# A linear-attention and channel-mixing kernel: weight conversion without clamps, a range test on a second load of the weights, and a new order table

## The chip, the cores and the metric

The kernel runs on one core of a Trainium2 chip. The metric is device time in microseconds (us) of one execution, median of the runs. Five engines take part: TensorE (PE, matmuls; PEld is its weight load), VectorE (DVE), ScalarE (ACT), GpSimd (POOL) and SyncE (SP), which here only issues DMAs. Every engine works through its own queue in order; semaphores hold an instruction until what it needs is there, and all that stands behind it on that engine waits too.

## What is computed

A decaying outer-product state per head, then two mixing layers per batch:

```python
for t in range(S):
    cur = np.einsum('bhd,bhe->bhde', u[None] * kt, vt)
    y[:, :, t] = np.einsum('bhd,bhde->bhe', rt, state + cur)
    state = wt[:, :, :, None] * state + np.einsum('bhd,bhe->bhde', kt, vt)
# x: y laid out as (B, S, H * D)
xt = x.transpose(0, 2, 1)
h = xt @ U @ V
u = x + h.transpose(0, 2, 1)
ch = np.maximum(u @ w_ch1, 0.0) @ w_ch2
return u + ch
```

Batch 4, 8 heads, 768 steps, head size 48, width 384, hidden width 1536, rank 32. U, V, w_ch1 and w_ch2 come to the device as 64-bit floats and are turned into pairs of float32r values (a high and a low part) on the device.

## The kernel before

**The recurrence** is cut into 24 chunks g of 128 steps (four batches of six). For a chunk: DMAs load w, r and k (`rk`), v and, from batch 1 on, a second layout of r and k (`kr`). DVE scans the decays backwards (step F) and forwards (step Q), scales r and k by them (RP and KS, on DVE or POOL) and forms the u term (PR; from batch 1 RK, RU and RED). ACT or POOL spread that term on a diagonal (SEL, lines 445 and 447). PE makes the scores (AM, line 507), DVE merges them with the diagonal under a mask (CP, line 510), PE turns k (KT), adds to the state (DS), and writes y (YA lines 566 and 576, YZ lines 589 and 593). ZA and ZM (lines 538, 547, 549) carry the state Z from chunk to chunk. XE, XT and XN bring y into the two layouts that follow.

**The mixing** of a batch needs all its six chunks: PE sums them with U (`gb`), ACT and DVE split that sum (GS, then GSL at line 668), and PE adds the product with V to x, giving u for two blocks of 384 steps (`hp`, line 723). u is split into a high and a low part (lines 735 to 741). Then per block 12 UP groups (line 782, nine matmuls each into one of three PSUM tiles of the tag `ffn`), a ReLU that splits the hidden value (HH line 789 on ACT or 791 on DVE, HL line 795 on DVE), 12 DN groups (line 817), the sum with u (line 832) and the store.

**The weights.** Each of the 24 pieces of w_ch1 and w_ch2 (128x384, 384 KB as 64-bit floats) goes through one of seven `raw` tiles: the load, AB (line 247, ACT: magnitude of the upper word), E (line 260, ACT: lower word), C1 (line 264, DVE: clamp to the range that can be converted), C2 (line 271, DVE: shift), SG (sign; line 279 on ACT or 281 on DVE), ADD (line 288, DVE or POOL: the float32 value), HI (line 329 or 331) and SUB (line 336, DVE or POOL). U and V take the same way once each. The `raw` tiles are also what u is written to.

**The order.** Every step is listed in a table, `ORDER`, three characters a step: which step comes next, whether it runs on its second engine, and how many warm-up matmuls (line 178, 52 instructions in all, on scratch data) PE gets in front of it. The program is issued in that order, so the table sets each engine's queue, SP's too. Tile pools are small: two for w, four for `rk`, two for v, seven for `raw`.

**Range tests.** GUARD (line 411, ACT, with an accumulated output) and the totals of the decay test w. Shortly before the end their results are summed (lines 955 to 964) and all engines branch: inside the range the kernel is done, outside it a slow general path computes everything anew. The inputs timed here stay inside.

Of the kernel before, what the change touches and what calls it, by code (L numbers as in the profile page):

```python
# [39 lines left out]
def channel_order():  # L40
# [14 lines left out]
    "0W00c05T00X05U05P05Y14K10d00f03i03n00V04904N03t03j05V03p00Y10Z04L10a03q00g01b03u11c00e00h10K00F04O00b1110120"
    "4Z01301A03vM3w04Y04P03r03s01J03-00M00i00l05W13m03o11404z01e01500G01f03x11C01L03y00j04i10k14b03zG3+0161170400"
    "1d04h01g11h04+01t01801914104jC1K01M05604k043G4404g01i04n04T05714o04d04204e04a05p00L00N01j14f04l00n04m14c10O0"
    "1N05004U01u01w04Q05801O15904R01P15204p84q02900P14544604V04W65301Q01R14S11v01B04X01x01y13l05q05z14uC5514r24v0"
    "5y05405+06945s05E05A01D00Q05B14w01E05x10R00S05-04s02R01S08O05u05114t05F01F11k05v00m00o06A04-01G15C05D06015d6"
    "5e05J65w00p08R01z06115Z01H01I10q15G20r11+08T01-08Y05a18o05H02A06228X05b15c02006305K08y05Q05L04x04y02C05t18U0"  # L60
    "8Z00s00t02S05fC2B01U05h05I06B02D05M22T05g05N02E15i01T08P08z15r08a15j08p08b05k05l09h05m01V08W18V08Q06C02I09O0"
    "8r02a08c11W02U08t05n05o06408d16506602F02V08g08u01X18q06701Y06802W16D08v06E06F06G08+02K06H09g00I08e08f08x06I0"
    "6M01Z08S16J08-06N00J02X16R06S08w09208h09309008i02Y19409j08s18j06O06P06K06L06V02Z06T06U08k06Q09609P11a09F07M0"
    "1l07N02J02c09101n02L02M09508l02G02H01o06r06s06t02N12O16c06d02P09l06e09E02Q06W06X00u09G09Q19R01m06o06Y06p09H0"
    "9m09n19I12102306Z06a00v06q06b02200x09706u06v06w09J00y09K09p07101p17201q09L09q06l06m00w02s07302400z10+09M09r1"
    "6f01r01s16g06h0AY06n00-01019s09t09o19W09S19T09X09909A09B02512b0Ai02d0Ab02-02e09U0AZ06+0261270281AG02j09812t0"
    "9V0Ad02v06i06x02f0Ae0Aj16j02w06k09b09c09Y09y02g0Ag19i09w09u09v12u02x17406y09d0750Af09z0A109Z09k19a0D40A202h0"
    "2i02k02m09x02n09N02y12z0Ao09+02+16z0380Ak13903B03C09-06-0DU07009e02l02o12p12q12r03003203107O07Q0Ac1760A603Z0"
    "Al0330Am03A09f03D17U07707V03H03J0A90AB0A70780AE19C09D07903413507A07B0Ah0360370An13E03F07C07R07D07S13I07T1A80"
    "3b03a0Ap07E07F0AM03G07G03Q03c07W07P0Aa0AA17X17e08003d03K0AC0AD03L0D303M0AN08103R0AH1AI03N08203O07f1AO0AQ03e1"  # L70
    "3P08m08n0AJ07g03T03U03S03V0830D60DD0AF0DT0840850AK1AL13f03W13X13Y07H03g1E307b07c1DE1A017h07i17j0AP03h07I07J0"
    "7K0DW07L07k07l07m07q0E40DB0D71D807r17s07t0D90A30E507d07Y0E607u17v0AR0AS0Db1DA1DY0DZ0DF0DG0A40DC0A50Dd0De1Dv0"
    "EV0AT0AU0AV0DX17Z07a0D50Dc0Da0Df1DL0Aq0Ar0As0AW0AX0DH1DI1Dy0DM07z0DJ0DK0EL07n07w07x0EM0D+07o1Dg0At0Au0Dl0DN0"
    "7p0Av0Aw0Ax0D-0DV0Dw0E017+17-0DP07y0E20Ay0Az0860870A+0A-0B00B10B20B30B40B51B60EO0Hu0En0Ew0880B70E70Dz08908C0"
    "8D08E08A08B0C10B80EW1B91EQ0EU0ER0EP18F08G0Dh1Di0Dm0C20FD0Dj0EX1E80EY0C30BA18I0E108J08K0BZ0Dx0FN0ES1Ba0Bb0Dk0"
    "8L08M08N0Eo0BH0BI0BJ0BK08H0C50BN0C60C71DQ0E90EA0BL1BM0BQ0DO0ET1BO1BP0Dn0Eq0EB0EC0Ev0BR1Do0BS0Dq0Dr0Ds0F10BB0"
    "BC1C90Bf0CA0F20Ed0EZ1Es0FO0Bg1Bh0EG0Et0Dp1EH0ED0EN0Hl0CB1BD0CC0Eb0BE0Bi0Bc0BF1EE0BG0EF0Bl0Eu0EI0Ec0FM0Bj1Bk0"
    "FG0I80Ea1Ee0BW0BX0EJ0EK0FI0Ef0FE0F30BY0Ep0Eg0Ei0FP0Ej0FF0FQ0FR1FS1DR0DS0Bd0BT0BU1Er0BV0FJ0FK1Bm0Bn0Be0Bo0Hk0"
    "FH0Hn0Ht0Br0Bp0Ex0Ey1Hv0Hw0Hs0Bs0Bt0Dt0Hp0Bu0C41Ez0E+0Bx0By0Bq0Hq0Hr0Bz0Hx0Ik0C81CP0CQ0FL0IB0E-0B+0F00I90IG0"
    "ID0Bv0Bw0IE0CR0F40B-0Ce0CM0CN1Cf1CO0Du0Cg0F50FT0FU0II0C00IJ0IK0IO0IP0Cb0Ia0Ek0Cc0CG0CH1CI0Eh0F60F70CV0Il0Im1"  # L80
    "CJ0CK0H+0H-0CL0F80F90IC0I00IL0Ib0IA0JA0JB0Ij0FA0Cd0IF0FV0FW0Hy1FB0FC0Hz1Id0CY0CZ0Ca0Ii0CW0CD0CE0CF0IH0Ck0Cl0"
    "If0Ig0Cm0El0Em0CS0Ih1J10FX0Ch0FY0I10Ie0CT0CU0FZ0Hm0I20Fa0Fb0Ci1Cj0IQ0I30IM0CX0I40IS0IN0JC1IR0Fc0Is0Fd0In0Io0"
    "Cn0Fe0Ff0Jc0J00J30J81Gi0JS0Ic0J41IT0IU0J50Gj0Co0Cp0Cq0Ct0Fg0Cu0J60Fh0Fi0Fj1Cv0Cw0Fk0Cr0Cs0Cz0Ip0It0Fl0Fm0Fo0"
# [959 lines left out]
```

## Time and profile before

| | us |
|---|---|
| median of 3 runs | 460.49 |
| lowest, highest | 459.89, 461.44 |
| the profiled execution | 460.15 |
| its span, first to last instruction | 458.4 |
| lies around the span | 1.75 |

The profile is one execution. "Busy" is the time in which an engine had an instruction under way; neighbouring instructions overlap a little, so what one costs its queue is the distance from its start to the next start, which the chain of waits shows directly. The profiled execution is 0.34 us under the median.

### The profile page before, as it was taken

Reading aid. Unit: us, or ns where it says so; the run is one execution under the profiler, and the core shown is the slowest. Engines: PE = TensorE matmul, PEld = TensorE weight load, DVE = VectorE, ACT = ScalarE, POOL = GpSimd, SP = SyncE. Lnnn points to the kernel's source line nnn. Section 1 sums busy time; section 2 is a strip of 40 time slices with the busy share of each in tenths; the row PEclk is TensorE's granted clock in tenths of the full one; section 3 lists DMA queues with packets and bytes.
Section 4 is the critical chain, followed back from the end, with each engine's and each line's share of the span. In section 5 each row is a group of like instructions: output and inputs, shape, how many; then the busy total and the mean of one; then the engine's idle time right before and its main releaser. Section 6 shows DMA issues by size and latency. Waiting matters only on the chain.

```text
span 458.4 us, 9721 instructions
## 1 busy us (share of the span) xinstructions
PE 442.2 (96%) x4066; PEld 409.9 (89%) x4066; DVE 296.7 (65%) x529; ACT 175.1 (38%) x434; POOL 104.5 (23%) x99
## 2 busy tenths in 40 slices
PE   4998899999999999999999999999999999999996
PEld 3675668999999899899999799999998899999995
...
GB/s 271 378 133 216 281 238 61 177 288 160 147 76 127 180 62 115 67 90 82 147 42 167 59 61 64 20 123 54 23 18 1 1 17 19 2 39 31 0 3 54
DMA packets 20497, 46.95 MB, mean 102 GB/s; under 512 B 2400, under 2 KB 8928, under 8 KB 20448
## 3 DMA queue, kind: packets, MB, share of 16 engines
...
q8 instruction: 33, 0.54, 0.5%
...
## 4 chain that ended last, share of the span: by engine, by line
PE 85%; DVE 7%; ACT 3%; DMA 2%; issue 1%; SPq 1%; DVEq 0%; ACTq 0%
PE f L782 33%; PE f L817 33%; PE aps L507 4%; PE y L566 2%; PE trk L495 2%; PE y L576 2%; PE trx L626 2%; PE y L589 1%; PE dS L517 1%; DMA rk<-in_rkT 1%; DVE A L510 1%; PE hp L723 1%; PE ga L649 1%; DVE Q L395 1%; PE idle L178 1%
## 5 line engine op out<-in xcount | busy, mean ns | idle before, releaser
L782 PE MATMUL f<-u,w1h 128*128 128x384 f32 x576 | 150.1, 341 | 0.7 <-ACT xT L745 0.7
L782 PEld LDWEIGHTS f<-u,w1h 128*128 128x128 f32 x576 | 103.7, 188 | 1.3 <-ACT xT L745 1.0
L817 PE MATMUL f<-hh,w2h 128*128 128x384 f32 x288 | 99.1, 344 | 0.0
L782 PE MATMUL f<-u,w1l 128*128 128x384 f32 x288 | 97.5, 339 | 0.0
L817 PE MATMUL f<-hh,w2l 128*128 128x384 f32 x288 | 97.4, 338 | 0.0
L817 PE MATMUL f<-hl,w2h 128*128 128x384 f32 x288 | 97.0, 337 | 0.0
L795 DVE SCALAR_TENSOR_TENSOR hl<-f,hh 128x384 fp32r<-128x384 f32 x96 | 52.4, 553 | 41.0 <-ACT hh L789 39.8
L789 ACT ACTIVATE hh<-f 128x384 fp32r<-128x384 f32 x47 | 23.1, 494 | 142.7 <-PE f L782 142.6
L817 PEld LDWEIGHTS f<-hh,w2h 128*128 128x128 f32 x288 | 54.1, 188 | 1.2 <-DVE hl L795 0.6
L817 PEld LDWEIGHTS f<-hl,w2h 128*128 128x128 f32 x288 | 54.5, 189 | 0.4
L782 PEld LDWEIGHTS f<-u,w1l 128*128 128x128 f32 x288 | 54.0, 188 | 0.0
L817 PEld LDWEIGHTS f<-hh,w2l 128*128 128x128 f32 x288 | 54.0, 187 | 0.0
L791 DVE TENSOR_SCALAR hh<-f 128x384 fp32r<-128x384 f32 x49 | 27.1, 554 | 33.4 <-PE f L782 33.4
L832 DVE TENSOR_TENSOR xT<-f,xT 128x384 f32<-128x384 f32 x24 | 13.0, 550 | 36.9 <-PE f L817 36.9
L510 DVE COPY_PREDICATED A<-maskf,aps 128x1024 f32<-128x1024 uint32 x24 | 32.7, 1361 | 2.8 <-PE aps L507 2.4
L445 ACT ACTIVATE A<-ident,dv 128x128 f32<-128x128 f32 x108 | 34.0, 394 | 1.2 <-DVE dv L435 1.2
L382 DVE TENSOR_TENSOR_SCAN F<-w,resets 128x517 f32<-128x517 f32 x24 | 30.7, 1281 | 4.4 <-DMA w<-in_wT 4.4
L395 DVE TENSOR_TENSOR_SCAN Q<-w,qd 128x516 f32<-128x516 f32 x24 | 31.1, 1295 | 0.2
L741 POOL TENSOR_TENSOR u<-xT,u 128x384 fp32r<-128x384 f32 x9 | 10.3, 1153 | 82.9 <-DVE u L737 63.8
L507 PEld LDWEIGHTS aps<-rk 48*128 48x128 f32 x384 | 23.3, 187 | 5.6 <-issue 3.9
L507 PE MATMUL aps<-rk 48*128 48x128 f32 x384 | 27.9, 285 | 0.5 <-DMA raw_w<-in_w 0.4
L407 POOL TENSOR_TENSOR rk<-rk,F 128x512 f32<-128x512 f32 x13 | 17.1, 1317 | 47.4 <-DVE F L382 27.5
...
## 6 DMA issues: line engine op xcount, KB each, us to landing
...
raw_w<-in_w SPq DMA_DIRECT2D x24, 384.0 KB, 5.5
kr<-in_rkN SPq DMA_DIRECT2D x18, 384.0 KB, 3.9
...
```

Of the source, the lines that this page charges most:

```text
L382: nc.vector.tensor_tensor_scan(out=F[:, ::-1], data0=st["w"][:, ::-1], data1=resets[:, ::-1], initial=1.0, op0=ALU.mult, op1=ALU.add)
L395: nc.vector.tensor_tensor_scan(out=st["Q"], data0=st["w"][:, 0:n], data1=qd, initial=0.0, op0=ALU.mult, op1=ALU.add)
L407: ENG[eng].tensor_tensor(out=rk[:, 1], in0=rk[:, 1], in1=F5, op=ALU.mult)
L445: nc.scalar.activation(A[:, i, j], ident, AF.Copy, scale=dv[:, NP * i + j : NP * i + j + 1])
L507: nc.tensor.matmul(aps[:, i, j, :], rk[r, 1, j, :], rk[r, 0, j, :], start=True, stop=True)
L510: nc.vector.copy_predicated(flat(st["A"]), mask8, flat(st["aps"]))
L782: nc.tensor.matmul(ps, wt[:, f, ct, :], u[ct][:, z], start=(n == 0), stop=(n == 8))
L789: nc.scalar.activation(hh, d["ps", f], AF.Relu)
L791: nc.vector.tensor_scalar(out=hh, in0=d["ps", f], scalar1=0.0, scalar2=None, op0=ALU.max)
L795: nc.vector.scalar_tensor_tensor(out=hl, in0=d["ps", f], scalar=0.0, in1=hh.bitcast(F32), op0=ALU.max, op1=ALU.subtract)
L817: nc.tensor.matmul(d["o", ct], wt[:, 4 * ct + part, f - 3 * part, :], hid[f][z], start=(part == 0 and n == 0), stop=(part == 3 and n == 8),)
L832: nc.vector.tensor_tensor(out=o, in0=d["o", ct], in1=o, op=ALU.add)
```

## The change

The 24 weight pieces lose step C1: `c1 = ab if not clamped`, so C2 follows AB. U and V keep it. Instead, each piece is loaded a second time later in the run (LC, SP, into a `raw` tile) and two ACT instructions with accumulated outputs (RT) sum up its magnitudes, and what they lack to the lower bound, into `sums`. The DN group 3.1.1.0, the eighth from the end, comes after all tests. The final vote gets two more columns: one reduction and two comparisons on DVE more. The general path converts the weights again with the clamps. And the order table is new: it moves steps on every engine, chooses other second engines, and asks for 63 warm-up matmuls.

```diff
 ORDER = (
-    "4704A04G00000100304804C00704B10200400514D04H10603k00800A05O04F10905X00B00C15R04IG4J04MA0D00H80EO5S14E00T00U0"
...
+    "4V04e04Y05m00000105p05v04W04a00300204b04600400514f14gS5r04c04d10S00T00V00U00605s04Z10700800A00a00904h00W10b0"
...
+    two = const.tile([P, 1], F32, name="two")
+    nc.vector.memset(two, 2.0)
...
-    def split_raw(key):
+    def split_raw(key, exact=False):
...
-        c1 = step(
+        clamped = exact or kind in ("U", "V")
+        c1 = ab if not clamped else step(
             "C1 " + nm, "DVE",
             lambda: nc.vector.tensor_scalar(
                 out=d["a"], in0=d["a"], scalar1=2.0, scalar2=122880.0 * 65536.0, op0=ALU.max, op1=ALU.min
...
+    sums = const.tile([P, 2, 2 * NF], F32, name="sums")
+
+    def test_raw(kind, i):
+
+        d, nm, braw = {}, f"{kind}{i}", Buf("raw")
+        q = i + (kind == "w2") * NF
+
+        def load():
+            t = stage.tile([P, TB, 2], U32, tag="raw", name=f"again_{kind}_{i}", bufs=RAW_BUFS)
+            nc.sync.dma_start(t.rearrange("p n t -> p (n t)"), (w1 if kind == "w1" else w2)[i].bitcast(U32))
+            d["high"] = t.bitcast(F32)[:, :, 1]
+
+        def sizes():
+            x = d["high"]
+            nc.scalar.activation(x, x, AF.Abs, scale=2.0**16, accum_out=sums[:, 0, q : q + 1])
+            nc.scalar.activation(x, x, AF.Relu, scale=-1.0, bias=two, accum_out=sums[:, 1, q : q + 1])
+
+        l = step("LC " + nm, "SP", load, ready[kind, i], take=[braw])
+        tests.append(step("RT " + nm, "ACT", sizes, [l], use=[braw]))
...
-        step("GUARD " + nm, "ACT", check_w, [lw], use=[buf["w"]])
+        tests.append(step("GUARD " + nm, "ACT", check_w, [lw], use=[buf["w"]]))
+        tests.append(st["tots"])
...
+                last = tests if nm == "3.1.1.0" else []
                 prev = step(
-                    "DN " + nm, "PE", down, [prev] + [s for f in fs for s in hs[f][1:]] + ready.get(("w2", 4 * ct + part), []),
+                    "DN " + nm, "PE", down, last + [prev] + [s for f in fs for s in hs[f][1:]] + ready.get(("w2", 4 * ct + part), []),
...
+        for key in pieces[2:]:
+            split_raw(key, exact=True)
...
+    for key in pieces[2:]:
+        test_raw(*key)
...
+        nc.vector.tensor_reduce(out=per[:, 2:4], in_=sums, op=ALU.add, axis=AX.X)
...
+        nc.vector.tensor_scalar(out=per[:, 2:3], in0=per[:, 2:3], scalar1=122880.0 * 65536.0, scalar2=None, op0=ALU.is_lt)
+        nc.vector.tensor_scalar(out=per[:, 3:4], in0=per[:, 3:4], scalar1=0.0, scalar2=None, op0=ALU.is_le)
```

Lines of the changed kernel are shifted by some 25, so 668 becomes 694, 741 becomes 767 and so on.

The first place is DVE's queue from GSL of batch 0 (out `gs`) up to the last low part of u that the first UP needs. Before:

```order
L668 TENSOR_TENSOR gs<-gb,gs 32x384
L435 TENSOR_REDUCE dv_994<-kr_769 128x8
L317 TENSOR_TENSOR Vst<-vm_187,Vst 32x384
L510 COPY_PREDICATED A_890<-maskf,aps_940 128x1024
L331 CAST w2h<-cva_w_3_788 128x384
L382 SCALAR_TENSOR_TENSOR F_1031<-w_976,resets 128x517
L549 TENSOR_TENSOR Z_1034<-dS,tots 128x384
L741 TENSOR_TENSOR u_0_1_1036<-hp_0_1_988,u_0_1_1036 128x384
L741 TENSOR_TENSOR u_0_0_992<-hp_0_0_974,u_0_0_992 128x384
L741 TENSOR_TENSOR u_0_2_1043<-hp_0_2_999,u_0_2_1043 128x384
```

and after (L432 is KS of chunk 7, L575 ZM, L753 the sum for block 1, L763 and L767 the split of u, L773 the copy that frees a PSUM tile):

```order
L694 TENSOR_TENSOR gs<-gb,gs 32x384
L432 TENSOR_TENSOR rk_816<-rk_816,F_903 128x512
L575 TENSOR_TENSOR Z_1039<-dS,tots 128x384
L753 TENSOR_TENSOR xT_1_761<-hp_1_0_1030,xT_1_761 128x384
L763 CAST u_0_0_1053<-hp_0_0_896 128x384
L767 TENSOR_TENSOR u_0_0_1053<-hp_0_0_896,u_0_0_1053 128x384
L773 COPY xT_0_411<-hp_0_0_896 128x384
L767 TENSOR_TENSOR u_0_1_1063<-hp_0_1_1057,u_0_1_1063 128x384
L767 TENSOR_TENSOR u_0_2_1084<-hp_0_2_1068,u_0_2_1084 128x384
```

The reduction, the sum for V, the merge, a cast and the scan F have left the stretch; KS, the sum for block 1 and the split of the first u have come in.

The second place is SP's queue for chunks 3 and 5 (first number in a name: the chunk, or the piece of the weights). Before:

```order
L367 DMA v_0_320<-in_vN 128x448
L355 DMA w_3_324<-in_wT 128x517
L359 DMA rk_3_362<-in_rkT 128x1024
L237 DMA raw_w1_11_364<-in_w1 128x768
L367 DMA v_2_446<-in_vN 128x448
L355 DMA w_5_448<-in_wT 128x517
L237 DMA raw_w2_1_514<-in_w2 128x768
L373 DMA u_rep_116<-in_uB 128x384
L359 DMA rk_5_547<-in_rkT 128x1024
```

and after:

```order
L380 DMA w_5_373<-in_wT 128x517
L240 DMA raw_w1_0_427<-in_w1 128x768
L392 DMA v_1_445<-in_vN 128x448
L384 DMA rk_3_466<-in_rkT 128x1024
L240 DMA raw_w1_3_468<-in_w1 128x768
L392 DMA v_3_490<-in_vN 128x448
L240 DMA raw_w1_8_513<-in_w1 128x768
L240 DMA raw_w2_1_515<-in_w2 128x768
L392 DMA v_2_528<-in_vN 128x448
L384 DMA rk_5_594<-in_rkT 128x1024
```

The load of w for chunk 5 now stands in front of v of chunk 1 and `rk` of chunk 3; before, `rk` of chunk 3 and v of chunk 1 were issued ahead of it.

The third place is ACT's queue in the second block of batch 1, where ReLUs (`hh`) stand among other work. Before:

```order
L789 ACTIVATE hh_1_1_8_3054<-f1_1_1_8_3040 128x384
L789 ACTIVATE hh_1_1_2_3097<-f1_1_1_2_3087 128x384
L499 ACTIVATE kn_18_3105<-trk_18_3100 128x512
L411 ACTIVATE junk_114,guard_112<-w_20_3050,b_max_106 128x512
L609 ACTIVATE xT_2_1_3052<-y_16_3108 128x3x128
```

and after (L360 and L361 are the two halves of a test RT):

```order
L815 ACTIVATE hh_1_1_8_2922<-f1_1_1_8_2893 128x384
L360 ACTIVATE again_w2_4_2926,sums_125<-again_w2_4_2926 128x384
L361 ACTIVATE again_w2_4_2926,sums_125<-again_w2_4_2926,two_112 128x384
L360 ACTIVATE again_w1_0_2602,sums_125<-again_w1_0_2602 128x384
L361 ACTIVATE again_w1_0_2602,sums_125<-again_w1_0_2602,two_112 128x384
L815 ACTIVATE hh_1_1_2_2935<-f1_1_1_2_2903 128x384
```

Two tests, each behind a load of its own, have come between two ReLUs.

## Rows read from the trace of the kernel before

**Rows 1.** The page: busy time, share of the span and instructions of each engine.

```profile
PE 442.2 (96%) x4066; PEld 409.9 (89%) x4066; DVE 296.7 (65%) x529; ACT 175.1 (38%) x434; POOL 104.5 (23%) x99
```

**Rows 2.** Busy us (count) by stretch: PE PEld DVE ACT POOL, clock, DMA share, GB/s.

```profile
0.00:20.00 20.00, 13.51 (x76) 9.62 (x76) 17.48 (x38) 14.38 (x36) 2.28 (x8) 1.00 0.90 328
...
7.84:66.38 58.54, 53.65 (x704) 39.28 (x704) 56.97 (x102) 54.23 (x135) 19.46 (x15) 1.00 0.72 252
...
74.00:453.00 379.00, 378.96 (x3261) 364.26 (x3262) 227.61 (x403) 112.25 (x278) 78.00 (x72) 1.00 0.24 76
```

**Rows 3.** Warm-up matmuls up to 74 us, both sizes (busy, mean ns).

```profile
L178 PE MATMUL idle<-w2l 128*128 128x512 f32 x43 | 16.1, 481 | 3.8 <-DVE w2l L172 3.8
...
L178 PE MATMUL idle<-w2l 128*128 128x256 f32 x9 | 3.1, 339 | 0.0
```

**Rows 4.** The chain of waits, 66 to 97 us: start, length, engine, line.

```profile
66.38 0.57 DVE gs L668
...
67.43 0.65 PE hp L715 x2
68.08 0.17 PE hp L723
...
71.36 0.94 DVE u L741 x2
...
73.58 0.39 ACT xT L745
...
74.02 2.04 PE f L782 x10
...
91.94 4.77 PE f L782 x27
```

**Rows 5.** The same chain, 40 to 45 us: steps of DVE's queue.

```profile
40.92 0.60 DVE rk L402
41.53 1.15 DVE F L382
42.67 0.25 DVE cva_w L264
42.93 0.47 DVE cva_w L288
...
44.26 0.47 DVE Z L538
```

**Rows 6.** The timeline, DVE 39 to 58 us, and one POOL instruction beside it.

```profile
39.63 0.69 DVE L463 TENSOR_TENSOR kr<-rk 128x512 f32<-128x512 f32 x1 [1.43 <-DMA rk<-in_rkT]
...
48.68 0.36 DVE L271 TENSOR_SCALAR cva_w<-cva_w 128x384 uint32<-128x384 uint32 x1
...
54.28 0.95 DVE L549 TENSOR_TENSOR Z<-Z,tots 128x384 f32<-128x384 f32 x1
55.15 1.17 DVE L271 TENSOR_SCALAR cva_w<-cva_w 128x384 uint32<-128x384 uint32 x1
56.24 1.33 DVE L510 COPY_PREDICATED A<-maskf,aps 128x1024 f32<-128x1024 uint32 x1
57.46 0.54 DVE L538 TENSOR_TENSOR Z<-dS,Z 128x384 f32<-128x384 f32 x1
...
54.79 1.31 POOL L428 TENSOR_TENSOR kr<-kr 128x384 f32<-128x384 f32 x1
```

**Rows 7.** Waits of SP's queue up to 76 us (total, times, longest).

```profile
SPq L355 <- DVE Q L395: 12.0, 6, 3.2
```

**Rows 8.** DMA issues, 100 to 400 us: count, size, median us from issue to landing.

```profile
raw_w<-in_w SPq DMA_DIRECT2D x3, 384.0 KB, 5.0
```

**Rows 9.** ACT's groups of instructions (busy, mean ns, idle before).

```profile
L789 ACT ACTIVATE hh<-f 128x384 fp32r<-128x384 f32 x47 | 23.1, 494 | 142.7 <-PE f L782 142.6
...
L411 ACT ACTIVATION_READ_ACCUMULATOR junk<-w,b_max 128x1 f32 x24 | 4.7, 196 | 0.0
```

More of the change, by code (lines that the diff above doesn't have):

```diff
@@ L53 @@
 ORDER = (
-    "4704A04G00000100304804C00704B10200400514D04H10603k00800A05O04F10905X00B00C15R04IG4J04MA0D00H80EO5S14E00T00U0"
[L55 to L83, printed above, removed]
@@ new lines @@
+    "4400c00X00Y04F04905n05w10d04i14A10Z14804B05t04kW4l04504G14w00B04C00e10f04D04E15304x00C10D00y00z00-02K04j11C0"
+    "0g04HI4I04J05L01401E04m60+04z04-04n01011101600h05415200EW4L24M05004+14K11S04NC4O00F01201311U01D04701i01k00HA"
+    "6B05105O01F01T01V01j01l01G05505604R44S04P04Q15u10K00M059A1m11W01H05q15A01I04X04r20I05M00i04s64t05V11X01Y01J1"
+    "5N06E05W05X00L04o04p01K01y05716F15815Q04y04u04v05Y05P11Z15T10j06K05R01n05BY5C04q00k06G05Z15D04T04U00N05S10l0"
+    "0m10n16H06C06L15U01+05E01M00G00J05GC5c06MG6N10o01o06J05a05b05d05F10O01p16I06X06O00p18m08p05H05I05-01506001z0"
@@ new lines @@
+    "Kb0Kd0Kc0Ke0Hj03-0Ht0Kf0Kg0Kh0Hu0Hw0Hx0Ki0Kj0Kn0Hy0Hz0Kk0Kl0Ko0Kp0Kq0H+0Hv0H-0Kr0Ks0I00I10I20Kt0Ku0Km0L20L30"
+    "L40L80L91LA0LH0L50L61L70I30I403z0Ky0LI0LJ0K-0L01L10KP0Kv0Kw0LQ03d0LR0Kz1Kx0K+0LB0LC0LD0LN0LO1LE0LF0LP0LT0LG0"
+    "Ll0Lm0LS0Ln1LU0LK0LL0410Lp0Lq0LM0LV0LW0LZ0La0Lb0Lo0LX0Lt0Lu0Lc0Lf0Lg0Ld0Lh0Lr1Lv0Li0Lw1Le0Ls1MD0ME1MF0Lj0MM0"
+    "M40M51M10M60M21M30Lk0MP0LY0MQ1MR0M70M80M90MA0MN0MO0MG0MH0Lx0MB1MC0Ly1Lz0L+0L-0M00MJ0MV0MW0MK1ML0MS0MI0MT0MX0"
+    "MU0MY0Mb0Mc0Md0Me0Mf0Mh0Mi0MZ0Mg0I50Mj0Mk0Ml0Ma0Mm0"
@@ L339, in split_raw @@
         ready[key] = [hi, sub]
+    sums = const.tile([P, 2, 2 * NF], F32, name="sums")
[12 more added lines that the diff above has]
+        tests.append(step("RT " + nm, "ACT", sizes, [l], use=[braw]))
+    tests = []
     sts = {}
@@ L904, in general @@
         del steps[:], ups[:], keeps[:]
+        for key in pieces[2:]:
+            split_raw(key, exact=True)
+        for s in steps:
+            s.run()
+        del steps[:]
         with tc.For_i(0, B, 1) as b:
@@ L949, in rwkv_moe_kernel @@
         spare.left += 1
-    per = const.tile([P, 2], F32, name="per")
+    per = const.tile([P, 4], F32, name="per")
     low = const.tile([1, 1], F32, name="low")
@@ L956, in test @@
         nc.vector.tensor_reduce(out=per[:, 1:2], in_=tots, op=ALU.min, axis=AX.XY)
+        nc.vector.tensor_reduce(out=per[:, 2:4], in_=sums, op=ALU.add, axis=AX.X)
         nc.vector.tensor_scalar(out=per[:, 0:1], in0=per[:, 0:1], scalar1=0.0, scalar2=None, op0=ALU.is_le)
         nc.vector.tensor_scalar(out=per[:, 1:2], in0=per[:, 1:2], scalar1=DECAY_MIN, scalar2=None, op0=ALU.is_ge)
+        nc.vector.tensor_scalar(out=per[:, 2:3], in0=per[:, 2:3], scalar1=122880.0 * 65536.0, scalar2=None, op0=ALU.is_lt)
+        nc.vector.tensor_scalar(out=per[:, 3:4], in0=per[:, 3:4], scalar1=0.0, scalar2=None, op0=ALU.is_le)
     def vote():
         cnt = psT.tile([P, NP, P], F32, tag="tr", name="cnt")
-        nc.tensor.matmul(cnt[0:1, 0, 0:2], ones, per, start=True, stop=True)
-        nc.vector.tensor_reduce(out=low, in_=cnt[0:1, 0, 0:2], op=ALU.min, axis=AX.X)
+        nc.tensor.matmul(cnt[0:1, 0, 0:4], ones, per, start=True, stop=True)
+        nc.vector.tensor_reduce(out=low, in_=cnt[0:1, 0, 0:4], op=ALU.min, axis=AX.X)
         nc.vector.tensor_scalar(out=flag, in0=low, scalar1=P - 0.5, scalar2=None, op0=ALU.is_lt)
```

40 lines of the change are left out of this document (30 added, 10 removed).

## The prediction

> **What bounds the kernel now.** The page's busy shares come first and mislead: PE is busy 96% of the span [rows 1], which seems to leave nothing to gain. The windows by stretch show two kernels in one [rows 2]. From 74 to 453 us PE is busy 378.96 of 379.00 us: matmuls stand end to end, and no other engine is waited for. Up to 74 us PE looks busy too, but 52 of its instructions there are warm-up matmuls on scratch data, 16.1 + 3.1 = 19.2 us of it [rows 3]; the first UP cannot start before batch 0 has gone through its recurrence. There DVE is the bound: between 7.84 us, where its first PR starts, and 66.38 us, where GSL starts, it is busy 56.97 of 58.54 us, and ACT 54.23 [rows 2]. The chain of waits agrees: DVE up to GSL, then a relay of PE, ACT and DVE to the first UP at 74.02 us [rows 4].
>
> So the time is three terms: when the first UP starts, the matmuls that are left then, and a tail behind them, the sum and the store of the last tile, that the change leaves alone. I count the PE instructions in front of the first UP in both programs: besides the warm-ups they are the same, but for one XT (three transposes, 0.33 us on the chain) that now comes earlier. What PE has left shrinks by 0.33 us, and all else must come from the start of the first UP.
>
> **C1 and what fills its place.** 12 of the 24 C1 stood in DVE's queue before GSL. A C1 costs its queue 0.25 us [rows 5], so 12 x 0.25 = 3.0 us leave the bound. The other 12 lie under the dense matmuls, where DVE is busy 227.61 of 379 us [rows 2], and are worth nothing. But the new table does not hand these 3.0 us over; it spends them. Counting DVE's steps before GSL in both orders: three RP and one KS go to POOL or behind GSL (4 x 0.60 us, as L402 [rows 5]), two ZM go to ACT (2 x 0.47, as L538 [rows 5]); with C1 that is 6.3 us out. In come three ADD, three SG and three SUB (9 x 0.47, as L288 [rows 5]), two RK and a RED (an estimate of 0.47 each from the same row, equal width), the second sum for V (0.57, as the equally formed GSL [rows 4]), a copy of totals (0.1) and one more merge CP (1.22, from L510's start to the next [rows 6]): 7.5 us in. Net the queue up to GSL grows by 1.2 us.
>
> One of its scans, F of chunk 4, moves ahead of the first PR into time in which DVE stood idle behind the load and the magnitude of U: -1.15 us [rows 5]. Its w is loaded ahead of `rk` of chunk 1, which delays that PR by 258 KB at 328 GB/s [rows 2], 0.8 us. Together GSL would start at 66.38 + 1.2 - 1.15 + 0.8 = 67.2 us with the stalls of before.
>
> **Stalls.** Before had 1.43 us of waiting for `rk` of chunk 5 at 39.63 us, and two instructions that took 0.95 and 1.17 us beside a POOL operation [rows 6]; against 0.54 for an equal sum and 0.36 for an equal shift that is another 1.2. Of these 2.6 us some go: `rk` of chunk 5 is now needed later, after two more SUB, a ZM and the other C2. But SP's new order makes others. The load of w of chunk 5 has to wait for a w tile, that is for a scan Q (such waits come to 12.0 us before [rows 7]), and now v of chunk 1, `rk` of chunk 3 and, behind further waits for `raw` tiles, `rk` of chunk 5 stand behind it. These stalls no row shows; bounds are none at all (GSL starts at 64.6 us) and all of before's (67.2). I take the middle, 65.9: the new order has the slack of some 10 steps between those loads and their use, and each load lands some 5 us after issue [rows 8]. ACT carries three SG and four SEL pieces less and eight ZM pieces, two HI, a GUARD and an E more, about +1.2 us by the same kind of count, and had 58.5 - 54.2 = 4.3 us free: no new bound, but little cover.
>
> What the skill says speaks against part of this. Beside POOL's L428 the DVE's shift took 1.17 us and not 0.36 [rows 6]. The Trainium skill ("SBUF — State Buffer", section "Who interferes with whom") has a DVE instruction with two SBUF inputs and a GpSimd instruction that reads SBUF shut each other out for a whole instruction. By that rule the nine added ADD, SG and SUB can be held up as the C1, which read one input at double rate, could; were three of them held 0.5 us longer than I count, GSL would start 1.5 us later. The trace agrees that such holds happen, and does not show these.
>
> **From GSL to the first UP.** Before this took 74.02 - 66.95 = 7.07 us: behind GSL in DVE's queue stood RED, a sum, a merge, a cast and a scan F, so the low parts of u started only at 71.36 us, and ACT's copies that free the PSUM tiles ended at 73.97 us [rows 4]. Now DVE does KS (0.60), ZM (0.47), the sum for block 1 (0.47), and high part, low part and copy of the first u (some 0.44 + 0.47 + 0.44): u is ready and a PSUM tile free 2.9 us after GSL. PE is later: two `hp` products (0.6 us), KT of chunk 7 which waits for KS (ends at 1.1 us), two pairs of `hp` matmuls (2 x 0.82, as 0.65 + 0.17 [rows 4]), an XT (0.33), the scores of chunk 7 (1.09) and a DS (0.49): 4.6 us. So the first UP starts at 65.9 + 0.57 + 4.6 = 71.1 us instead of 74.02. From there the remaining low parts of u (DVE at about 3.9 us) are in time, and the matmuls stay dense if DVE and ACT keep up as before.
>
> **Second loads, tests, vote.** 24 x 384 KB more at a DMA share of 0.24 [rows 2]; 48 ACT instructions that cost the queue an estimated 0.55 us each with the read of their accumulator (0.494 for a ReLU of equal width and 0.196 for such a read, less the overlap of neighbours [rows 9]), 26 us in all, on an engine that sat 142.6 us waiting for UP results alone [rows 9]. The vote adds a reduction and two comparisons under DN groups. Cost in the sum: nothing, with the matmuls as cover; without it, see the second rival.
>
> **Sum.** 74.02 - 71.1 = 2.9, plus 0.33: 3.3 us. From the profiled execution 460.15 that is 456.9; the median lies 0.34 us above it, so **457.2 us**. Without stalls 1.3 us less (455.9), with all of before's 1.3 more (458.5).
>
> **Rivals.** *No gain.* The w load in front of v and `rk` holds up chunk 3 for more than the table allows: then kr of chunk 3, DS and Z of chunk 1 come late, and the state chain passes it on to GSL. A delay of 2.9 us over my GSL eats all but the transpose: 460.2 us. For it: DVE and ACT are both nearly full, and 9 more two-input steps stand beside POOL. Against: the load is issued as soon as Q of chunk 2 ends, some 5 steps of 1.2 us ahead of its first use.
>
> *Slower.* The tests hold up ReLUs. In ACT's queue a test waits for its own load; an HH behind it waits too. UP groups come every 1.59 us (4.77 for three [rows 4]) and three PSUM tiles allow HH and HL two groups of delay, 3.2 us, less some 0.5 each of their own [rows 9]: 2.2 us of slack. A load that is issued just ahead of its test lands 5.0 us later [rows 8]: 2.8 us of PE standing. Some eight of the 24 tests have an HH right behind them; from two such cases on the gain is gone (3.3 / 2.8 = 1.2), with half of the eight it is 457.2 + 4 x 2.8 = 468 us. For it: SP's queue is in order, and a second load needs a free `raw` tile that u also takes. Against: most second loads stand tens of SP rows ahead of their tests, and ACT idles between tests.
>
> **How the numbers follow.** Measurement tells about 0.3% from no change, 1.4 us: faster is below 459.1, slower above 461.9. My forecast, 455.4 to 458.0: 0.54. The same with before's stalls kept or a little worse, 458.0 to 459.1: 0.17. Better than 455.4, if DVE's waits vanish and its queue is shorter than counted: 0.04. No gain, 459.1 to 461.9: 0.14. Slower by the tests: 0.11. So faster 0.75, same 0.14, slower 0.11. The range runs from 454.9, a further 1 us under the sum without stalls, to 460.2, the case without gain; it leaves out the slower case, a few hundredths below, and the upper part of no gain, about 0.18.
>
> **What would show it.** In the profile after: first UP near 71 us (right between 69.8 and 72.4); GSL ending near 66.5, so that most of the gain lies between GSL and UP and not in front of GSL; no C1 among the weight lines; PE without a gap from there to about 450 us. Wrong if GSL comes after 69, if the waits of PE name an HH or HL behind a test, or if PE idles where chunk 3's loads land.

## The result and the profile after

The change made the kernel slower: 463.65 us median (462.57 to 465.96) against 460.15 (459.35 to 461.44), ten runs each, ratio 1.0071 with a 95% interval of 1.0053 to 1.0089. The forecast was 457.2 with a range from 454.9 to 460.2, so both its sign and its range were wrong. The profiled execution of after took 463.77 us, a span of 462.0; it is set against the one of before, 460.15. (The ten runs put before's median at that same 460.15, so the 0.34 us that the forecast added for the median came from three runs alone.)

The page's line of busy time answers to [rows 1]:

```profile
PE 446.5 (97%) x4077; PEld 413.5 (89%) x4077; DVE 287.7 (62%) x507; ACT 208.2 (45%) x540; POOL 93.2 (20%) x94
```

PE is busy 4.3 us more, ACT 33 us more (the tests), DVE 9 us less. That tells nothing yet of where time is lost. The windows of after do; they are cut at its first PR (8.43), GSL (68.78) and first UP (74.28). Columns as in [rows 2]: busy us and count of PE, PEld, DVE, ACT, POOL, granted clock, DMA share, GB/s.

```profile
8.43:68.78 60.35, 56.53 (x758) 42.74 (x760) 56.80 (x98) 54.09 (x142) 16.21 (x15) 1.00 0.71 239
68.78:74.28 5.50, 4.96 (x57) 3.63 (x53) 4.14 (x8) 3.17 (x9) 1.86 (x2) 1.00 0.94 366
74.28:100.00 25.72, 24.57 (x212) 22.60 (x210) 24.58 (x42) 20.66 (x48) 15.42 (x13) 1.00 0.52 158
100.00:340.00 240.00, 240.00 (x2207) 229.40 (x2206) 152.89 (x260) 102.25 (x273) 53.88 (x53) 1.00 0.39 130
340.00:370.00 30.00, 29.43 (x359) 25.97 (x358) 13.71 (x23) 11.80 (x33) 0.85 (x1) 1.00 0.10 33
```

And one window of before, which [rows 2] held only as a part of 74 to 453 us:

```profile
74.00:100.00 26.00, 25.98 (x273) 24.79 (x274) 25.04 (x50) 22.37 (x51) 9.49 (x9) 1.00 0.56 187
```

Read DVE's column. Up to GSL its work is what it was, 56.80 us against 56.97 [rows 2], but the stretch is 60.35 us long and not 58.54: it waits 3.55 us where it waited 1.57. Behind the first UP PE now has holes in two windows. And in the 26 us behind the first UP, DVE of before is busy 96%: it had next to no slack there to follow an earlier start.

The ledger, in us of the two profiled executions:

| | before | forecast | after |
|---|---|---|---|
| first PR on DVE | 7.84 | 8.6 | 8.43 |
| GSL starts | 66.38 | 65.9 | 68.78 |
| GSL to first UP | 7.64 | 5.2 | 5.50 |
| first UP starts | 74.02 | 71.1 | 74.28 |
| first UP to the start of the last matmul | 379.70 | 379.4 | 383.07 |

So the miss of 6.9 us (456.9 forecast for this execution) is 2.9 us at GSL, 0.3 in the relay behind it and 3.7 behind the first UP.

**GSL.** The waits of DVE from 20 to 60 us (start, length, line, in brackets the idle time and its releaser):

```profile
23.59 0.56 DVE L292 CUSTOM_DVE_ANT_0 cva_w<-raw_w,cva_w 128x768 uint16<-128x768 uint16 x1 [0.67 <-ACT raw_w L283]
33.02 0.69 DVE L489 TENSOR_TENSOR kr<-rk 128x512 f32<-128x512 f32 x1 [0.93 <-DMA rk<-in_rkT]
45.15 0.17 DVE L501 COPY dv<-trd 128x8 f32<-128x8 f32 x1 [0.52 <-PE trd L494]
57.32 0.56 DVE L454 TENSOR_TENSOR kr<-kr 128x384 f32<-128x384 f32 x1 [0.93 <-DMA kr<-in_rkN]
```

Before's 1.43 us for `rk` of chunk 5 [rows 6] are gone, and four waits stand in their place. Two are loads, and the first of those is `rk` of chunk 3, which SP now issues behind the load of w of chunk 5. SP's waits up to 76 us (total, times, longest) show what it stood for, 20.9 us on scans Q where it had been 12.0 [rows 7]:

```profile
SPq L380 <- DVE Q L420: 20.9, 5, 6.3
```

Two holds are of another kind, instructions that ran long beside one on POOL:

```profile
60.83 0.99 DVE L340 TENSOR_TENSOR w1l<-cva_w,w1h 128x384 fp32r<-128x384 f32 x1
67.02 1.26 DVE L292 CUSTOM_DVE_ANT_0 cva_w<-raw_w,cva_w 128x768 uint16<-128x768 uint16 x1
```

The SUB at 60.83 us ran beside SEL on POOL (60.61, 0.80 long), where the SUB at 64.81 took 0.55. The ADD at 67.02 ran beside RP on POOL (66.68, 1.19 long), where the ADD at 64.36 took 0.53. Together that is 1.2 us, as much as the two long instructions of before [rows 6], and the same two steps run long in e3, e7 and e8. Both ADD and RP have two inputs in SBUF. The Trainium skill ("SBUF — State Buffer", section "Who interferes with whom") has the two engines shut each other out there; the trace agrees, with 1.26 us for 0.53.

**Behind the first UP.** PE waits three times:

```profile
PE trk L521 <- POOL rk L432: 0.6, 1, 0.6
PE trx L652 <- ACT xT L635: 0.6, 1, 0.6
PE f L808 <- DVE hl L821: 0.4, 1, 0.4
```

From start to next start these come to 0.75 (KT, at 88 us), 0.73 (XT, at 351 us) and 0.59 us (UP, at 81 us) more than usual, 2.07 together. None of them ends on a test. The one at 351 us ends on XE, which waited for a store to free its tile. The chain of waits shows how those at 81 and 88 us hang together, and that the chain does not pass over to PE at the first UP (74.28) as it did at 74.02 before [rows 4]:

```profile
73.90 1.02 DVE u L767 x2
74.92 0.80 DVE cva_w L275 x3
75.73 0.47 DVE kr L454
...
76.21 1.23 DVE F L407
...
79.55 1.24 DVE Q L420
...
80.82 0.77 POOL cva_w L292
...
81.99 5.49 DMA rk<-in_rkT
...
87.65 1.20 POOL rk L432
...
88.89 0.66 PE trk L521 x4
```

DVE still works off chunk steps and weight pieces, without a gap from 73.90 us on; the low half for PE at 81 us stands behind them. An ADD on POOL comes late, with it a free `raw` tile, with that SP gets past a weight load to `rk` of chunk 8, then KS, then PE at 88 us. Ahead of it all a load was late: AB on ACT waited for a weight piece, and the low parts of u on DVE waited for ACT, 1.26 us:

```profile
72.51 0.55 ACT L250 ACTIVATE cva_w<-raw_w 128x384 f32<-128x384 f32 x1 [1.08 <-DMA raw_w<-in_w]
73.90 1.02 DVE L767 TENSOR_TENSOR u<-hp,u 128x384 fp32r<-128x384 f32 x2 [1.26 <-ACT u L761]
```

The other 1.3 us (383.07 less 379.70, less 2.07) are no wait at all: the same matmuls stand in an order that takes longer, below.

### The profile page after: what moved, and what is told of

The parts are those of the page before. It is cut to its first block, busy times and chain, and to the rows that moved or that the text cites. A ratio compares the mean times of both kernels' runs of the same rounds, so it can differ in the third digit from the quotient of the medians.

```text
span 462.0 us, 9851 instructions
## 1 busy us (share of the span) xinstructions
PE 446.5 (97%) x4077; PEld 413.5 (89%) x4077; DVE 287.7 (62%) x507; ACT 208.2 (45%) x540; POOL 93.2 (20%) x94
## 4 chain that ended last, share of the span: by engine, by line
PE 86%; DMA 8%; DVE 3%; SPq 1%; issue 1%; ACT 1%; POOL 0%; POOLq 0%; ACTq 0%; DVEq 0%
PE f L843 33%; PE f L808 30%; PE aps L533 4%; DMA rk<-in_rkT 4%; PE y L592 3%; PE idle L179 2%; PE y L602 2%; PE y L615 2%; PE trk L521 2%; PE dS L543 2%; PE trx L652 1%; PE trd L494 1%; DMA kr<-in_rkN 1%; DMA raw_U<-in_U 1%; PE ga L675 1%; PE y L619 1%
## 5 line engine op out<-in xcount | busy, mean ns | idle before, releaser
L815 ACT ACTIVATE hh<-f 128x384 fp32r<-128x384 f32 x56 | 27.0, 489 | 110.5 <-PE f L808 110.5
L817 DVE TENSOR_SCALAR hh<-f 128x384 fp32r<-128x384 f32 x40 | 22.1, 554 | 36.2 <-PE f L808 36.1
L473 POOL TENSOR_SCALAR_AFFINE_SELECT A<-dv 128x512 f32<-128x512 f32 x23 | 16.6, 724 | 103.4 <-PE y L602 60.6
L471 ACT ACTIVATE A<-ident,dv 128x128 f32<-128x128 f32 x100 | 31.7, 394 | 1.7 <-DVE dv L461 1.7
L767 POOL TENSOR_TENSOR u<-xT,u 128x384 fp32r<-128x384 f32 x12 | 13.3, 1112 | 74.3 <-DVE u L763 42.0
```

What stands on the lines that cost most here:

```text
L471: nc.scalar.activation(A[:, i, j], ident, AF.Copy, scale=dv[:, NP * i + j : NP * i + j + 1])
L473: nc.gpsimd.affine_select(out=A[:, i], in_=dv[:, NP * i : NP * i + NP].unsqueeze(2).broadcast_to([P, NP, P]), pattern=[[0, NP], [1, P]], c ...
L815: nc.scalar.activation(hh, d["ps", f], AF.Relu)
L817: nc.vector.tensor_scalar(out=hh, in0=d["ps", f], scalar1=0.0, scalar2=None, op0=ALU.max)
```

## The experiments

The table's characters tell a reader nothing, so edits of it are shown by step names, on one engine.

### The parts of the change, one by one

e1: clamps alone taken out, in the order of before:

```diff
-        c1 = step(
+        clamped = kind in ("U", "V")
+        c1 = ab if not clamped else step(
```

> The table of before, with the 24 weight clamps C1 dropped from it and nothing else moved; the weights' range is neither clamped nor tested, so this kernel leaves that guard out. Theory order (the new table costs the time, the clamps alone are a gain): 12 C1 of 0.25 us leave DVE's queue ahead of GSL; GSL starts 1.5 to 3.0 us ahead of before's 66.38, and the kernel takes 457.2 to 458.7 against 460.15. Rival load-bound (DVE's queue waits for loads and for other engines anyway): GSL moves by less than 0.7 us and the kernel takes 459.5 to 460.5.

Measured: 459.89 us against 460.18, ratio 0.9992 (0.9977 to 1.0008). One of its twelve executions took 1095.51 us; it is left out of the ratio, and what happened there is not known. GSL did come 1.95 us earlier, at 64.43, but the first UP only 0.97, at 73.05. The window up to GSL gives the price of a clamp: DVE is busy 54.26 us where it was 56.97 [rows 2], 2.71 us less for 12.

```profile
7.89:64.43 56.54, 52.39 (x700) 38.62 (x701) 54.26 (x91) 52.88 (x133) 17.96 (x15) 1.00 0.74 259
```

DVE's rows show who took the rest:

```profile
64.43 0.56 DVE L669 TENSOR_TENSOR gs<-gb,gs 32x384 fp32r<-32x384 f32 x1
68.27 1.68 DVE L383 TENSOR_TENSOR_SCAN F<-w,resets 128x517 f32<-128x517 f32 x1 [0.49 <-DMA w<-in_wT]
...
72.65 0.56 DVE L742 TENSOR_TENSOR u<-hp,u 128x384 fp32r<-128x384 f32 x1 [1.32 <-ACT u L736]
```

The scan F of chunk 9 now waits for its w, and the low parts of u stand behind it. Behind the first UP everything is as before (379.64 us). GSL came as early as the order theory had it; the time is the rival's, and no gain is shown.

e2: the whole change in the order of before; the 48 steps of the tests go in behind the same UP and DN groups as in after:

```diff
-ORDER = (the table of after)
+ORDER = (the table of before, 24 x C1 dropped, 24 x LC and 24 x RT put in)
```

> The whole changed program, second loads, tests and wider vote included, in the order of before: C1 dropped from it and each second load and test put behind the same UP or DN group as in the changed kernel. Theory order: the same time as without tests within 0.6 us, since matmuls cover them. Rival tests (9.4 MB of second loads and 48 more ACT instructions hold PE up): 1.3 to 3.5 us over the run without tests.

Measured: 461.64, ratio 1.0029 (1.0015 to 1.0042), 1.75 us over e1, as the rival had it. PE has one wait, and ACT's queue shows why: at 249.89, 251.19 and 252.50 us tests stand in a row, 1.30 us each, ahead of an XN and an XE (ACT first, then PE):

```profile
252.50 0.54 ACT L360 ACTIVATE again_w<-again_w 128x384 f32<-128x384 f32 x1
...
253.16 0.63 ACT L361 ACTIVATE again_w<-again_w,two 128x384 f32<-128x384 f32 x1
...
253.79 0.47 ACT L656 ACTIVATE xn<-trx 128x384 f32<-128x384 f32 x1
254.16 0.48 ACT L635 ACTIVATE xT<-y 128x384 f32<-128x384 f32 x1
```

```profile
254.70 0.55 PE L652 MATMUL trx<-ident,xT 128*128 128x128 f32 x3 [1.50 <-ACT xT L635]
```

e3: after without the tests:

```diff
-    for key in pieces[2:]:
-        test_raw(*key)
```

> The changed kernel in its own order, without the second loads, the tests and their part of the vote; the weights' range is not tested at all, that part is left out. Theory order: 463.0 to 463.7, as the three waits of PE behind the first UP (80.7, 88.1, 351 us) end on a low half, a chunk's load and an xT tile and not on a test. Rival tests: 460.5 to 462.0.

Measured: 464.49, ratio 1.0081 (1.0056 to 1.0107): no faster than after. Nor does the fall of the clock in its profile (last section) hide a gain: its three runs with a mean granted clock of 0.998 and more took 463.43 to 464.22 us, those of after 462.57 to 463.77. In the new order the tests are not what costs. Against e1, which but for a few small set-up instructions differs from it by the table alone, it is 4.6 us slower.

e4: after with the clamps back:

```diff
-        clamped = exact or kind in ("U", "V")
+        clamped = True
```

> The changed kernel with the 24 clamps put back, each right ahead of its shift C2. 12 of them stand ahead of GSL. Theory load-bound (in the new order DVE waits for loads): GSL, at 68.78 in the changed kernel, moves by less than 1.0 us and the kernel takes 463.6 to 464.6. Rival queue (DVE's queue is the bound): GSL comes 12 x 0.25 = 3.0 us later, the kernel takes 466 to 467.

Measured: 470.09, ratio 1.0208 (1.0179 to 1.0238), outside both ranges. GSL came at 74.44, 5.7 us behind after's and 3.4 behind e3's 71.06, so the direction is the queue theory's. The price of a clamp can't be read from it: the granted clock fell as in e3 up to 24 us (last section), but here a further time ahead of GSL, and DVE is busy 62.98 us up to GSL where it is 56.94 in e3, twice what 12 clamps of 0.25 us explain.

```profile
60.00:65.00 5.00, 3.78 (x38) 2.20 (x42) 4.54 (x7) 2.34 (x8) 2.14 (x2) 0.67 0.01 3
```

### Is DVE the bound behind the first UP too?

e5: one scan moved in e1, on DVE:

```diff
 HI w2 3
-F 9
 ZM 6
 ULP 0.0.1
 ULP 0.0.0
 ULP 0.0.2
+F 9
```

> The order of before without the weight clamps (as the run that gave 459.89), and one step moved: the scan F of chunk 9 goes behind the low parts of the first u in DVE's queue. Weights are neither clamped nor tested here. Theory relay (what stands between GSL and the first UP on DVE sets when the matmuls begin: F waited 0.49 us for a w load that took 6.83, ran 1.6 us, and the low parts of u came behind it): first UP some 2 us ahead of 73.05, at 70.5 to 71.5, and the kernel takes 457.4 to 458.4. Rival (the stalled scan moves its delay to chunk 9, and PE waits for it later): first UP early, but a PE wait behind it, 459.3 to 460.3.

Measured: 459.52, ratio 0.9985 (0.9971 to 0.9999); the last matmul starts 0.03 us later than in e1. The first UP came 0.77 us earlier, at 72.28, and it was given back:

```profile
77.55 0.62 PE L783 MATMUL f<-u,w1h 128*128 128x384 f32 x2 [0.24 <-DVE hl L796]
```

The DVE queue in front of that low half has no gap from 71.87 us on. A second matmul waits for a low half at 82.71 us, in the chain of waits behind F, Q and that low half on DVE. From start to next start the two holds are 0.41 and 0.29 us, 0.70 of the 0.77 that was won. The rival held: an earlier start of the matmuls is worth nothing while DVE has as much to do for the next ones.

e11 and e12: two hybrids, without clamps and tests, joined the orders at the first UP (some steps had to move so that the tile pools suffice, 24 in e11 and 3 in e12):

```diff
-ORDER = (the table of after)
+ORDER = (after's up to the first UP, then what is left, as before has it)     first hybrid
+ORDER = (before's up to the first UP, then what is left, as after has it)     second hybrid
```

> No clamps and no tests (the weights' range is neither clamped nor tested). The new order up to the first UP, all that is left in the order of before. Theory rest (of the 3.5 us that the change costs, the front gives 0.3 and the order behind it 3.2): first UP at 74.3, 380 us of matmuls behind it, 460.0 to 461.2. Rival backlog (the new front starts the matmuls with DVE's other work undone, so any order waits for it): PE waits behind the first UP, 462 to 464.

> No clamps and no tests (the weights' range is neither clamped nor tested). The order of before up to the first UP, all that is left in the new order. Theory rest: first UP at 73.1, 381 to 383 us behind it for the same matmuls, 461.0 to 463.0. Rival backlog: no waits behind the first UP, 459.5 to 460.5.

Measured: 476.49 and 467.71, ratios 1.034 and 1.0155. Both theories fell: what was meant to be "the rest" is no part that can be costed by itself. In e11 PE waited 5.8 us from 126 to 141 us, for XN, KN and a load of v, and the granted clock fell there:

```profile
120.00:140.00 20.00, 14.95 (x146) 11.77 (x144) 9.92 (x18) 4.79 (x9) 2.25 (x2) 0.68 0.43 138
```

In e12 a weight load that found no free `raw` tile in its old place came late: ACT waited 4.15 us for it, the shift behind that 3.15 us in DVE's queue, and the low half behind it held PE:

```profile
82.24 0.36 DVE L272 TENSOR_SCALAR cva_w<-cva_w 128x384 uint32<-128x384 uint32 x1 [3.15 <-ACT cva_w L247]
...
83.10 0.56 DVE L796 SCALAR_TENSOR_TENSOR hl<-f,hh 128x384 fp32r<-128x384 f32 x1
```

```profile
83.71 1.01 PE L783 MATMUL f<-u,w1h 128*128 128x384 f32 x2 [4.41 <-DVE hl L796]
```

### The loads and the matmuls' order in after

e7: five loads moved in after, on SP:

```diff
+v 1
+rk 3
 w 5
 raw w1 0
-v 1
-rk 3
 raw w1 3
 v 3
+v 2
+rk 5
 raw w1 8
 raw w2 1
-v 2
-rk 5
...
+rk 8
 raw w2 0
 raw w2 11
-rk 8
```

> The changed kernel, five loads moved in SP's queue: v of chunk 1 and rk of chunk 3 ahead of the load of w of chunk 5, v of chunk 2 and rk of chunk 5 ahead of the weight pieces w1 8 and w2 1, rk of chunk 8 ahead of w2 0. Theory loads (SP's in-order queue made GSL late and one of the PE waits): the waits of DVE for rk_3 (0.87) and kr (0.93) and the wait of PE at 88.1 us (0.75) go, the kernel takes 461.2 to 462.7. Rival PE (the warm-up matmuls that fill PE in the first 30 us hold DVE): GSL moves by less than 0.5 us, 462.8 to 463.8.

Measured: 462.91, ratio 1.0062 (1.0039 to 1.0085), with runs from 461.22 to 464.44. The time lies in the rival's range and is not told apart from after's. The profile, of its fastest run (span 459.5), shows more: DVE's wait for `rk` of chunk 3 is gone, GSL comes 0.75 us earlier and the first UP 0.76, and both waits of PE at 81 and 88 us are gone. Of the 0.75 us, 0.29 are an earlier first PR (8.14), ahead of all that was moved; DVE idles 3.00 us up to GSL where it idled 3.55. PE's only wait from there on:

```profile
PE trx L652 <- ACT xT L635: 0.5, 1, 0.5
```

Two of DVE's four waits stay (1.32 for kr, now at 56.57 us, and 0.43 at 23.00), and a SUB waits 0.84 for ACT. Loads are part of the cause, not all. Behind the first UP they are more of it: the low parts of u no longer wait, at 71.97 us, and PE follows without the two waits, with DVE busy 25.46 of the 26.48 us up to 100.

e13: from this kernel, 12 of the 19 KT and XT behind the first UP that another chunk step follows were put at the end of their block, where an FFN group follows (on PE, one place; on ACT four pairs of steps change places):

```diff
-XT 1.1
 DS 8
 AM 9
 YA 8
 YZ 8
+XT 1.1
```

> The changed kernel with the five loads moved ahead (462.91), and in 12 of the 19 places behind the first UP where a chunk's transposes KT or XT are followed on PE by scores, products or a state update, they go to the end of that block, so that an FFN group follows them. Theory adjacency (three transposes take 0.42 us up to the next start when such an instruction follows and 0.24 to 0.30 when an FFN group does): the matmuls from the first UP to the last DN take 380.87 us without waits in the base and 379.3 to 380.2 here. Rival (the extra is elsewhere): 380.6 and more. New waits, where KN or XN come later, are counted apart.

Measured: 463.76, ratio 1.0085. Inconclusive on the time: new waits of 3.0 us came in (1.1 of them on a low half). Without them the matmuls took 380.4 us against 380.9 in e7, between the two theories. The transposes alone went from 5.65 + 6.49 (KT + XT) to 5.21 + 6.09 us, start to next start, 0.84 less, of which some 0.5 are left in the sum of all matmuls. The same sums in the traces of before and after tell more: 5.13 + 5.92 against 5.71 + 6.50, 1.16 of the 1.3 us, with three XT fewer in after. Of the rest, the sums with U take 0.53 us more and the products for y 0.39 less. Before has 8 transposes with a chunk step behind them, after 19. The timeline of after, PE, start and length:

```profile
358.94 0.49 PE L652 MATMUL trx<-ident,xT 128*128 128x128 f32 x3
359.36 0.65 PE L592 MATMUL y<-A,v 128*32 128x128 f32 x16
...
361.03 0.55 PE L652 MATMUL trx<-ident,xT 128*128 128x128 f32 x3
361.33 0.42 PE L843 MATMUL f<-hh,w2h 128*128 128x384 f32 x1
```

Three transposes hold PE 0.42 us up to the start of a product with v and 0.30 up to that of a DN group; four (KT) 0.53 and 0.35.

### Where tests cost nothing

e6: tests apart from each other, in e5's order (on ACT, three of the 24 places):

```diff
 T 10
 KN 10
+RT w1 4
 HH 0.1.10
...
 XN 1.0
+RT w1 7
 E w2 10
...
 XE 10
+RT w2 11
```

> The whole changed program with second loads and tests, in the order of before without C1, F of chunk 9 behind the low parts of u, and the 24 tests apart from each other in ACT's queue (never four in a row as at 249 to 254 us of the earlier run, where PE then stood 1.65 us). Theory place (a test costs 1.3 us of ACT's queue and holds PE up only where several stand together ahead of an XN or XE): within 0.5 us of the run without tests, 457.5 to 459.0. Rival bandwidth (the second loads cost by themselves): 1.3 us and more over it.

Measured: 462.90, ratio 1.0057 (1.0039 to 1.0076), 3.4 us over e5. The place theory, as stated, fell. e10: the same with short tests:

```diff
-            d["high"] = t.bitcast(F32)[:, :, 1]
+            d["high"] = t.bitcast(F32)[:, 0:4, 1]
```

> The kernel with the tests apart (462.90), all second loads in place, but each test reads 4 of the 384 columns, so that ACT's two instructions become short; most of the range is not tested, that part is left out. Theory ACT's queue: most of the 3.4 us over the run without tests goes, 459.7 to 461.0. Rival loads: 462.3 to 463.1.

Measured: 459.80, ratio 0.9993 (0.9979 to 1.0007), as the theory had it. With all 9.4 MB of second loads in place it is 0.3 us over e5, less than the runs can tell; ACT's time costs the rest.

e9: all tests late, behind the last chunk's XN (on ACT, the first of them):

```diff
 XN 3.5
 G4 3
 GS 3
+RT w1 4
+RT w1 7
 UH 3.0.1
```

> The whole changed program in the order of before without C1 (nothing else moved there), all 24 second loads and tests put behind the last chunk's XN, between 350 and 420 us, where in before ACT is busy 3.5 of 40 us and the DMA share is 0.06. Theory ACT's queue (a test costs what stands behind it in ACT's queue while chunks are still going through): 459.6 to 460.5, no more than 0.5 us over the 459.89 of the same order without tests. Rival loads (the 9.4 MB cost PE by themselves, wherever they are): 461.2 to 463.

Measured: 463.27, ratio 1.0061 (1.0039 to 1.0083). Neither theory: one wait does most of it. On SP a second load waited 22.3 us for a `raw` tile in which u still stood, until PE had done its last UP with it. The load of w1 0, two places behind, was issued at 395.12 us and landed 5 us later; its test waited for it, and the ReLU behind the test held PE. SP's wait (total, times, longest), then ACT, then PE:

```profile
SPq L355 <- PE f L808: 36.9, 3, 22.3
```

```profile
400.18 0.54 ACT L360 ACTIVATE again_w<-again_w 128x384 f32<-128x384 f32 x1 [3.60 <-DMA again_w<-in_w]
...
401.47 0.47 ACT L815 ACTIVATE hh<-f 128x384 fp32r<-128x384 f32 x1
```

```profile
401.99 0.44 PE L843 MATMUL f<-hh,w2h 128*128 128x384 f32 x1 [2.17 <-ACT hh L815]
```

PE's standing cost more than the wait. Behind it the granted clock fell, as it did in e12 behind the wait of 4.41 us:

```profile
400.00:410.00 10.00, 7.86 (x34) 7.60 (x35) 1.12 (x2) 9.56 (x29) 0.00 (x0) 0.83 0.65 213
```

So e16 puts tests behind DN groups, with no ReLU and, but for one SEL at 320.70 us, no chunk step close behind, and their loads earlier in SP's queue (SP and ACT, one place):

```diff
+LC w1 4      (SP, in front of the store of block 1.1)
 OUT 1.1.2
...
 DN 2.0.0.0
+RT w1 4      (ACT)
 DN 2.0.0.1
```

> The whole changed program in the order of before without C1 (nothing else moved there); the 24 tests behind DN groups of blocks 2.0, 2.1 and 3.0, where no chunk's step and hardly a ReLU stands behind them in ACT's queue, their loads ahead of the stores on SP. Theory queue (a test costs only what waits behind it): 459.6 to 460.6, as without tests (459.89). Rival (31 us more of ACT cost wherever they are): 461.2 and more.

Measured: 459.31, ratio 0.9976 (0.9959 to 0.9994). The whole change, tests included, is as fast as e1, and PE has no wait behind the first UP. Its longest window:

```profile
100.00:340.00 240.00, 239.96 (x2230) 229.50 (x2229) 159.26 (x268) 88.85 (x236) 65.00 (x61) 1.00 0.33 109
```

e18 and e17: the same kernel again, and beside it one with the scan F of chunk 9 behind u, the edit shown for e5:

> The kernel with the tests in the gaps once more (459.31 before), beside the one with the scan moved. Theory queue: 459.0 to 459.7 and faster than before by 0.1 to 0.4%. Rival (the first look was luck): 459.8 to 460.6.

> The whole changed program in the order of before without C1, tests behind DN groups of blocks 2.0, 2.1 and 3.0 (459.31 so), and F of chunk 9 behind the low parts of the first u. Theory DVE (DVE is the bound up to some 100 us, so an earlier first UP is given back in a wait for a low half near 77 us): 459.0 to 459.6, with a PE wait of about 0.4 near 77 us. Rival (the gains add): 458.3 to 458.9 and no such wait.

Measured: 459.03, ratio 0.9967 (0.9941 to 0.9992), and 459.97, ratio 0.9988 (0.9971 to 1.0005). The version with the order of before, no clamps and tests in the gaps is the fastest found, some 0.3% ahead of before. The earlier first UP (73.18 against 73.33) again came back in waits, 0.5 us in two, the larger of them below. e17's time lies above both of its ranges, so the two gains do not add, as the DVE theory had it:

```profile
78.42 0.61 PE L808 MATMUL f<-u,w1h 128*128 128x384 f32 x2 [0.30 <-DVE hl L821]
```

### Warm-ups

e8 and e14: in after, the warm-ups ahead of MD 1 and KT 1 cut; and, again in after and alone, more ahead of MD 0 (numbers of 512 columns):

```diff
-MD 1: 7      KT 1: 8
+MD 1: 4      KT 1: 2.5
```

```diff
-MD 0: 4.5
+MD 0: 7.5
```

> The changed kernel with fewer warm-up matmuls ahead of two steps: 4 instead of 7 ahead of MD 1 and 2.5 instead of 8 ahead of KT 1 (the numbers of before), 8.5 fewer of 512 columns in the first 20 us. Theory PE (the warm-ups stand on the chain, all the more where the granted clock is 0.5): 461.0 to 462.5. Rival loads: less than 0.5 us off, 463.1 to 464.1. Rival clock (with fewer of them the granted clock falls more often): 464.5 to 466.

> The changed kernel with six more warm-up matmuls ahead of MD 0, in the place where PE stood idle from 14.3 to 16.4 us in the executions whose granted clock then fell to 0.5 from 17 to 24 us. Theory clock (that fall delays the merges and GSL by 2.3 us in part of the executions): mean granted clock of 0.997 and more in every run, spread below 2 us, median 461.5 to 463.0. Rival (the warm-ups only delay MD 0): median 464 to 465.5.

Measured: 464.50, ratio 1.0088 (1.0062 to 1.0114), and 464.41, ratio 1.0083 (1.0059 to 1.0108). Fewer did not help, and e8's number is that of the clock rival: all six runs have a mean granted clock of 0.990 to 0.995, and the profile has the fall that the last section tells of. What the warm-ups cost where the clock does not fall is thus not shown. More did not help either; the clock theory of e14 fell, with a mean granted clock of 0.989 and 0.991 in two runs of six. Its profile shows the granted clock at 0.70 from 10 to 12 us, in front of the place that was filled.

## Why the prediction was wrong, step by step

- **C1 and what fills its place: right.** 0.25 us a clamp in the queue; e1 against before has 2.71 us for 12, 0.23 each. The count of what comes in and goes out, +1.2 less 1.15, promised no change of DVE's busy time, and it is 56.80 against 56.97 us. First PR: 8.43 for a forecast of 8.6.
- **Stalls: the first step that failed.** The text took the middle between none and before's 2.6 us of waits and long instructions, 1.3, and let before's sum be the upper end. That is no bound for stalls made by another order of loads. After has 3.55 us of idle time and 1.2 of long instructions, 4.7 together; that makes GSL late, while the queue itself came out 0.3 us shorter than counted. The text had named the very load, w of chunk 5 ahead of `rk` of chunk 3, and put it among the rivals; e7 shows it and its like to be worth 0.55 us of DVE's idle time. The other waits (ACT, PE, kr) were in no sum.
- **From GSL to the first UP: right.** 5.50 us for 5.17, where it had been 7.64. e5 supports the lever: one scan less ahead of the low parts of u moved the first UP by 0.77 us; in e17 it was 0.15, no more than two profiles can tell apart.
- **"PE stays dense after": the second step that failed, and the larger one.** It rested on DVE being busy 227.61 of 379 us [rows 2]. That is an average over a tight stretch and a loose one: 25.04 of 26.00 in the first 26 us, 202.57 of 353 after. DVE has next to no slack up to about 100 us, so time won by letting u pass other DVE steps is owed to those steps. e5 and e17 gave back what they had won. In after two of the three waits of PE, 1.34 of 2.07 us, came on such a dense queue; what set them off were late loads, since e7 moved loads alone and has neither.
- **The same matmuls, 0.33 us fewer: right in the count, wrong in the cost.** 51 and not 54 XT transposes stand behind the first UP, but what follows a transpose matters: 1.3 us more without any wait, where the forecast had 0.33 less. The prediction counted instructions and not neighbours. That 1.16 us of it lie at the transposes is read from starts; e13 got 0.84 us back there and some 0.5 in all, so that the neighbours are the cause is in part argued.
- **Tests at no cost: right for this table, and not for the reason given.** A test takes 1.30 us of ACT's queue (31 us in all, forecast 26: 0.55 each for two), and e3 shows that after is no faster without them. "Matmuls as cover" does not follow from ACT's idle share, though: the same tests cost 1.75 us (e2) or 3.4 us (e6, e9) in other places, and nothing in e16.
- **The rivals.** "No gain" asked for a GSL 2.9 us behind the forecast, and that is what came, by luck: the load that it names made DVE wait 0.93 us, and the rest has other causes. It gave 460.2 and missed the 3.7 us behind the first UP. "Slower" did not happen in after, but e9 is its mechanism to the letter: a second load that waits for a tile which u takes, a test that waits for that load, a ReLU behind it, PE standing 2.17 us (forecast 2.8).

What stays open: of the 3.55 us that DVE idles ahead of GSL, e7 accounts for 0.55. And how much the fall of the clock described below adds to the median of after, whose runs spread from 462.57 to 465.96; that it does not make the loss is shown by the five with a mean granted clock of 0.998 and more, at 462.57 to 463.77, and by the profile, which has no fall up to its end.
